# Forgetting attention with a bilinear FFN on one core: one cumulative-sum chain for the forget gates, four heads per score group in the first batch, the second batch's decay on TensorE, idle matmul steps spread through the order, weights loaded later

## The chip, the core and the metric

The kernel runs on one core of a Trainium2 chip. The metric is device time in microseconds (us) of one execution. Times of the kernel before: 422.95, 422.79 and 419.99 us, median 422.79. The engines are called by the profile's names: PE is TensorE (PEld its weight loads), DVE is VectorE, ACT is ScalarE, POOL is GpSimd, SP is SyncE, which issues most of the DMAs.

## What is computed

Eight batches (B) of eight heads (H) with 576 positions (S) of 64 values (D) go through attention with a forget gate, and the result through a bilinear FFN with 4608 tokens, width 512 and inner width 1536.

```python
scores = scale * np.matmul(q, k.transpose(0, 1, 3, 2))
log_f = np.log(np.clip(f, 0.0001, 1.0))
cum = np.cumsum(log_f, axis=-1)
decay = cum[:, :, :, None] - cum[:, :, None, :]
scores = np.where(causal, -1000000000.0, scores + decay)
scores = scores - np.max(scores, axis=-1, keepdims=True)
attn = np.exp(scores)
attn = attn / (np.sum(attn, axis=-1, keepdims=True) + 1e-09)
attn_out = np.matmul(attn, v)
x = attn_out.transpose(0, 2, 1, 3).reshape(B * S, H * D)
a = x @ w_a
b = x @ w_b
out = a * b @ w_out
```

Within a row of the softmax the term cum of the query's own position is a constant, so the kernel only subtracts cum of the key's position.

## The kernel before

**Tiles.** A pair of heads is a tile t; a batch has four, so t runs from 0 to 31, and batch b holds t = 4b to 4b + 3. Two tiles are a unit u (half a batch, four heads). The 576 query rows of a head are cut into five blocks i = 0 to 4 of 128, 128, 128, 128 and 64 rows; block i needs keys 0 to 128(i + 1). Score groups g hold blocks (1, 0), (2), (3), (4) (`groups`, L371). The inner dimension of the scores is split in two halves of 32 (dh), so that a head uses 32 rows of TensorE and four heads can lie in its four row groups at once (`RG`, L67).

**An order written by hand.** The program first builds a list of steps (`op`, L123), each with the engines that it may run on, its function, and what it depends on. `ORDER` (L961) is the order in which all steps are issued, and `CHOICE` (L1068) gives one letter for each step that has a choice of engine. An engine works its own steps in this order; semaphores hold a step until its inputs are there and its buffer is free. So a step that waits holds everything that stands behind it on its engine, the issue of DMAs on SP and POOL included.

**Start.** `constants` makes an identity on POOL. `warming` (L171) has TensorE multiply it 60 times with itself into a bank that nobody reads. `f_load` (L193) loads f twice: once as 16 rows per head group repeated over 128 partitions (the form that TensorE needs: 16 (batch, head) rows in each of eight 16-partition groups, the first two batches), once as 64 rows (all heads and batches). Each copy has its own chain: `clip` on DVE, `log` on ACT, `scan` on DVE (the cumulative sum). The first copy goes on through `high_part` and `rows_part` (L218, L221) into `crow`, fp16 rows with a high and a low part; the second is stored to DRAM by `cum_store` (L225) and read back, spread over 128 partitions, for batches 2 to 7 (`load_spread`, L450).

**Batch 0 (`DIRECT`, L69).** `first_attention` (L766) works a tile at a time. `qk_group` (L382) computes the scores of two heads with q and k, adds -cum of the key by a matmul of `pick` with `crow` (L400, L421), and the causal mask by matmuls of `low` with `neg` (L403, L427). So decay and mask are in the score bank (PSUM) when it is read: `do_max` (L478, DVE) takes the maximum of each row there, `do_exp` (L528, ACT) the exponential with the row sum, both out of the bank. There are two score tiles of two banks each (tag `sc`) and four other banks (tag `ff`) for everything else: transposes, value products, FFN.

**Batch 1.** It has the mask by matmul, too, but the decay comes from VectorE. `spread_mm` (L436) multiplies `crow` over 128 rows, `spread_ev` (L444) evicts that to SBUF (eight evictions on ACT or DVE), `spread_tail` (L447) clears its tail on POOL. `do_decay` (L483, the profile's L504) adds the spread row to the scores on DVE, takes the maximum in the same instruction and writes the sum to an SBUF tile `S`, from which `do_exp` reads. A score bank is free when the additions of its tile are done.

**Batches 2 to 7.** As batch 1, but the spread row comes by DMA and carries the mask (`mask_copy`, `mask_tail`, `mask_last` on POOL).

**After the softmax.** `do_norm` (L549, the profile's L555) scales by the reciprocal of the row sum on POOL. The probabilities are transposed, in batch 0 by TensorE (`pe_tr`, L573, evicted by `pe_tr_evict`), later by DMA; `do_pv` and `do_pv4` (L586, L616) multiply with v, `do_ev` (L627) puts the result into `xT`.

**FFN.** `ffn` (L904) takes blocks of 256 to 512 tokens. For each of 12 slices of the inner width it makes `psa` and `psb` (four matmuls each, `ff_mm` L863), copies `psa` to fp16 (`ff_copy`), multiplies (`ff_mul`, L875, DVE), and then `pso` (L881) multiplies with w_out. The FFN steps of finished batches fill TensorE between the score groups of later ones.

**Weights.** `weights` (L353) issues seven loads on POOL, which convert to fp16: columns 0 to 512 and 512 to 1536 of w_a and w_b, and three parts of w_out. Before, the first three (w_a 0, w_b 0, w_a 512) are issued within the first 5 us; the first psa runs at 52.1 us.

Of the kernel before, what the change touches and what calls it, by code (L numbers as in the profile page):

```python
# [37 lines left out]
def kernel(  # L38
# [30 lines left out]
    DIRECT = 1  # L69
    EARLY = 2  # L70
    PSPREAD = range(NP, 2 * NP)
# [99 lines left out]
    def warming(_):  # L171
        p = ps.tile([128, 512], FP32, tag="ff", bufs=RING["ff"], name="idle")
        for n in range(60):
            nc.tensor.matmul(out=p[:, 0:128], lhsT=ident, rhs=ident, start=True, stop=True)
# [3 lines left out]
    if 60:  # L178
        take(op("E", "warm", warming, [o_id], 60), "ff")
# [4 lines left out]
    NR = [128, B * H]  # L184

    def f_tiles():
        x = [s_pool.tile([128, 1024], FP32, tag="S", name=n) for n in ("cum_f", "cum_l")]
        y = spread[RING["bc"] - 1].rearrange("p h x -> p (h x)")
        cw["f"] = x[0][:, 0:S], y[0:NR[1], 0:S]
        cw["l"] = x[1][:, 0:S], y[0:NR[1], S:2 * S]  # L190
        cw["1"] = x[0][:, S:].bitcast(FP16)[:, 0:S]

    def f_load(e, m):  # L193
        rows = f.rearrange("b h s -> (b h) s")
        if m == 0:
            rows = bass.AP(rows.tensor, 0, [[0, 8], [S, 16], [1, S]])
        ENG[e].dma_start(out=cw["f"][m], in_=rows)
# [8 lines left out]
    def clip(m, lo, hi):  # L206
        x = cw["f"][m][:, lo:hi]
        nc.vector.tensor_scalar(out=x, in0=x, scalar1=1e-4, scalar2=1.0, op0=MAX, op1=MIN)

    def log(m, lo, hi):  # L210
        nc.scalar.activation(out=cw["l"][m][:, lo:hi], in_=cw["f"][m][:, lo:hi], func=LN)

    def scan(m, lo, hi):
        x = cw["f"][m]
        nc.vector.tensor_tensor_scan(out=x[:, lo:hi], data0=cw["1"][0:NR[m], lo:hi], data1=cw["l"][m][:, lo:hi],
                                     initial=x[:, lo - 1:lo] if lo else 0.0, op0=MUL, op1=SUB)

    def high_part(lo, hi):  # L218
        nc.vector.tensor_copy(out=chigh[:, lo:hi], in_=cw["f"][0][:, lo:hi])

    def rows_part(lo, hi):  # L221
        nc.vector.scalar_tensor_tensor(out=crow[:, lo:hi], in0=chigh[:, lo:hi], scalar=lsel,
                                       in1=cw["f"][0][:, lo:hi], op0=MUL, op1=ADD)

    def cum_store(_):  # L225
        nc.sync.dma_start(out=cum_d, in_=cw["f"][1])
# [4 lines left out]
    f_users = take(o_f[1], f"bc{RING['bc'] - 1}")  # L231
    o0 = op("D", "ones", f_ones)
    o_w = op("A", "table", warm_table(LN), [o0])
    crow_ops, lns = [], []
    for m, parts in ((0, ((0, 256), (256, S))), (1, ((0, S),))):
        o3 = None
        for lo, hi in parts:
            a = (m, lo, hi)
            o1 = op("D", "fclip", lambda _, a=a: clip(*a), [o_f[m]], hi - lo)
            o2 = op("A", "fln", lambda _, a=a: log(*a), [o1, o_w], hi - lo)  # L240
            o3 = op("D", "fscan", lambda _, a=a: scan(*a), [o2, o0] + ([o3] if lo else []), hi - lo)
            lns.append(o2)
            mine = [o1, o2, o3]
            if m == 0:
                o4 = op("D", "fhi", lambda _, lo=lo, hi=hi: high_part(lo, hi), [o3], hi - lo)
                o5 = op("D", "frow", lambda _, lo=lo, hi=hi: rows_part(lo, hi), [o4, o_pick], hi - lo)
                crow_ops.append(o5)
                mine += [o4, o5]
            for u in s_users:
                u.extend(mine)  # L250
            if m:
                f_users.extend(mine)
    o6 = op("S", "stc", cum_store, [o3])
    f_users.append(o6)
    o_e = op("A", "table", warm_table(EXP), lns)
    o_low = op("D", "low", lows, [o0, o_pick])
# [860 lines left out]
```

## Time and profile before

| | |
|---|---|
| median of three runs | 422.79 us |
| the profiled execution's own time | 424.4 us |
| its span, first to last instruction | 422.6 us |
| mean granted clock of TensorE | 0.947 |
| matmuls | 3712 |
| HBM read, written | 52.35 MB, 9.58 MB |

The span is what the views of the trace divide up; 1.8 us of the execution lie around it. Lines of a timeline give the start and length in us, the engine, the line of the kernel, the operation, output <- input, shapes, the count, and in brackets how long the engine stood idle before and what ended it. Rows of windows give a stretch, its length, each engine's busy time and number of instructions, the clock that TensorE was granted as a share of full speed, the share of time that the 16 DMA engines were busy, and GB/s. Rows of lines give, behind the shapes and the count, the busy time in us, the mean ns of one instruction, and the idle time before. Rows of DMAs give the size and the median us from issue to landing. Ends of matmuls are modelled, so neighbouring matmuls overlap in the rows; the distance of starts is the better measure of their cost.

### The profile page before, as it was taken

To read this page: it belongs to the slowest core of one execution; us is meant where nothing else is said; L and a number is where in the kernel's file an instruction comes from. 1 tells how busy PE (TensorE), PEld (TensorE's weight loads), DVE (VectorE), ACT (ScalarE), POOL (GpSimd) and SP (SyncE) were. 2 spreads that over 40 slices of the span, in tenths; PEclk is the share of its full clock that TensorE was granted. 3 is DMA by queue.
4 is the path that set the end of the run, shared out by engine and by line. 5 is a ranking of instruction groups with operands and counts; after the bars stand their busy time and mean duration, and the time that the engine had idled before them with its cause. 6 is when DMAs were issued, how large, how long until landed. Compare 5 with 4: busy or idle time off the path is not lost. (4 is left out here: it accounts for less than half of the span.)

```text
span 422.6 us, 10576 instructions
## 1 busy us (share of the span) xinstructions
PE 393.6 (93%) x3712; PEld 210.9 (50%) x3712; DVE 323.4 (77%) x1020; ACT 255.5 (60%) x760; POOL 257.1 (61%) x436
## 2 busy tenths in 40 slices
PE   5379999988999998999999999999899999999996
PEld 5245677565664553545445444444344444444552
DVE  3977699989899998996887799786968985452450
ACT  2867689887676856675856576387556764111121
POOL 4479688978788668876793948496775745000000
PEclk9555599999999999999999999999999999999999
DMA  8999969999999999979979897979897907300201
GB/s 239 287 201 236 185 152 279 172 293 191 211 270 200 274 208 298 251 233 180 311 158 280 188 243 233 208 194 208 253 159 237 154 31 148 109 0 2 100 2 74
DMA packets 149390, 80.85 MB, mean 191 GB/s; under 512 B 130648, under 2 KB 133208, under 8 KB 149336
## 3 DMA queue, kind: packets, MB, share of 16 engines
q1 hardware_dynamic: 145424, 75.01, 74.0%
q0 software_dynamic: 3696, 4.72, 6.8%
q8 instruction: 29, 0.48, 0.5%
q10 hardware_dynamic: 216, 0.44, 0.4%
q14 instruction: 25, 0.20, 0.1%
HBM read 52.35 MB, written 9.58 MB: 147 GB/s over the span
## 5 line engine op out<-in xcount | busy, mean ns | idle before, releaser
L504 DVE CUSTOM_DVE_ANT_0 S<-sc,spread 128x384 f32<-128x384 f32 (+4 forms) x232 | 124.0, 562 | 15.5 <-PE sc L624 5.6
L866 PE MATMUL psa<-xT,wa 128*128 128x512 f16 (+2 forms) x528 | 115.7, 342 | 1.4 <-ACT a L137 1.2
L866 PE MATMUL psb<-xT,wb 128*128 128x512 f16 (+2 forms) x528 | 115.3, 341 | 1.4 <-DVE ht L877 1.0
L555 POOL TENSOR_SCALAR PA<-PA,st 128x128 f16<-128x128 f16 (+2 forms) x180 | 83.4, 478 | 40.5 <-DVE st L547 26.6
L537 ACT ACTIVATE PA<-S,st 128x256 f16<-128x256 f32 (+2 forms) x168 | 83.9, 501 | 27.3 <-DVE st L504 26.0
L886 PE MATMUL pso<-wout,ht 128*128 128x512 f16 x432 | 98.0, 380 | 0.1
L877 DVE TENSOR_TENSOR ht<-psb,a 128x512 f16<-128x512 f32 (+2 forms) x132 | 76.2, 587 | 22.1 <-PE psb L866 17.4
L137 ACT CAST a<-psa 128x512 f16<-128x512 f32 (+2 forms) x92 | 45.4, 498 | 50.9 <-PE psa L866 46.9
L389 PE MATMUL sc<-kT,qT 32*128 32x128 f16 (+5 forms) x960 | 55.4, 284 | 20.5 <-DVE qT L300 8.0
L866 PEld LDWEIGHTS <-wb 128*128 128x128 f16 x528 | 49.8, 98 | 45.6 <-issue 6.1
L866 PEld LDWEIGHTS <-wa 128*128 128x128 f16 x528 | 49.8, 98 | 45.0 <-issue 4.9
L555 POOL TENSOR_SCALAR PB<-PB,st 128x512 f16<-128x512 f16 (+1 forms) x90 | 62.7, 710 | 15.2 <-DVE st L547 9.6
L886 PEld LDWEIGHTS <-ht 128*128 128x128 f16 x432 | 40.8, 98 | 48.9 <-DVE ht L877 1.4
L537 ACT ACTIVATE PB<-S,st 128x512 f16<-128x512 f32 x56 | 40.1, 716 | 13.0 <-DVE st L504 10.9
L389 PEld LDWEIGHTS <-qT 32*128 32x128 f16 (+1 forms) x960 | 23.5, 99 | 48.2 <-issue 24.8
L537 ACT ACTIVATION_READ_ACCUMULATOR PA<-S,st 128x1 f32 x168 | 31.7, 189 | 0.0
L457 POOL TENSOR_SCALAR_AFFINE_SELECT spread<-spread 128x768 f32<-128x768 f32 x24 | 20.7, 866 | 15.3 <-DMA spread<-cum_d 15.3
L137 ACT COPY osb<-pso 128x512 f32<-128x512 f32 x20 | 11.6, 578 | 27.2 <-PE pso L886 26.3
L533 ACT ACTIVATE PB<-S,st 128x576 f16<-128x576 f32 x28 | 21.7, 774 | 9.2 <-DVE st L504 4.4
L141 DVE CAST a<-psa 128x512 f16<-128x512 f32 (+2 forms) x40 | 23.6, 592 | 3.5 <-PE psa L866 3.1
L547 DVE RECIPROCAL st<-st 128x2 f32<-128x2 f32 x128 | 18.8, 156 | 7.7 <-ACT PB L537 4.2
L504 DVE DVE_READ_ACCUMULATOR2_ANT st<- 128x1 f32 (+1 forms) x280 | 22.9, 82 | 0.0
(98 smaller groups left out, 432.7 us busy)
## 6 DMA issues: line engine op xcount, KB each, us to landing
spread<-cum_d SPq DMA_DIRECT2D x24, 576.0 KB, 6.3
out_dram<-osb SPq DMA_DIRECT2D x36, 256.0 KB, 3.0
k<-in_k_dram SPq DMA_DIRECT2D x15, 576.0 KB, 7.3
q<-in_q_dram SPq DMA_DIRECT2D x15, 576.0 KB, 7.0
v<-in_v_dram SPq DMA_DIRECT2D x32, 256.0 KB, 7.1
wout<-in_moe_w_out_dram POOLq DMA_DIRECT2D x3, 512.0 KB, 7.6
wa<-in_moe_w_a_dram POOLq DMA_DIRECT2D x1, 1024.0 KB, 22.8
v<-in_v_dram SPq DMA_DIRECT2D x8, 128.0 KB, 4.8
```

The lines of the kernel that those rows point to most:

```text
L137: nc.scalar.copy(out=out_, in_=in_)
L141: ENG[e].tensor_copy(out=out_, in_=in_)
L389: nc.tensor.matmul(out=dst, lhsT=lhsT, rhs=rhs, start=start, stop=stop, skip_group_check=True)
L457: nc.gpsimd.affine_select(out=c[:, :, 0:SM].rearrange("p h (j k) -> p h j k", k=128), in_=c[:, :, SM:2 * SM].rearrange("p h (j k) -> p h j ...
L504: nc.vector.tensor_tensor_reduce(out=o, in0=x, in1=y, scale=-1.0, scalar=3e38, op0=ADD, op1=MIN, accum_out=m)
L533: nc.scalar.activation(out=p_blocks(t, 4), in_=T[("s" if direct else "z", t, 4)], func=EXP, bias=st[:, 8:9], scale=sign, accum_out=st[:, 1 ...
L537: nc.scalar.activation(out=p_blocks(t, i)[:, :, h, :], in_=(T[("s", t, i)][:, h, :] if direct else T[("z", t, i)][:, h * n:h * n + n]).rea ...
L547: nc.vector.reciprocal(out=st[:, 20 + 2 * i:22 + 2 * i], in_=st[:, 10 + 2 * i:12 + 2 * i])
L555: ENG[e].tensor_scalar(out=p, in0=p, scalar1=st[:, c:c + 1], scalar2=1.0, op0=MUL, op1=MUL)
L866: nc.tensor.matmul(out=p[:, 0:n], lhsT=w16[:, db, 128 * fb:128 * fb + 128], rhs=xTflat[db][:, t0:t0 + n], start=(db == 0), stop=(db == 3))
L877: nc.vector.tensor_tensor(out=ht[:, 0:n], in0=T.pop(("psb", t0, fb))[:, 0:n], in1=T.pop(("a16", t0, fb))[:, 0:n], op=MUL)
L886: nc.tensor.matmul(out=o, lhsT=T[("ht", t0, fb)][:, 128 * tb:128 * tb + 128], rhs=wout16[:, fb, :], start=(fb == 0), stop=(fb == 11))
```

## The change

1. **One chain for f.** f is loaded into one tile: 64 partitions hold the first two batches repeated, as TensorE needs them, 64 partitions all heads and batches. The first load is issued by ACT, the second by SP, behind the first k load. One chain of clip, logarithm and scan, in two column parts, serves both halves. `rows_again` copies the 64 partitions of `crow` to the other 64 (first part on POOL, second on DVE).
2. **Batch 0 by units.** `qk_group` always takes four heads. The second unit's groups 0 to 2 go to four single `ff` banks instead of the two score tiles (`single`).
3. **Batch 1 direct.** `DIRECT = 2`: its decay comes by matmul with `pick` and `crow`, its maximum by `do_max`, and its exponential reads the score bank. Spread matmuls, their evictions, the tails and the additions of batch 1 are gone.
4. **Idle steps.** `warming` is replaced by 40 steps of `filler` with four 128-column matmuls each. In the new order 18 stand before the first score group, 13 between it and the second unit's first group, and 9 singly later, the last in the FFN's second token block.
5. **A new order and choice of engines** for the whole program. The steps that the text speaks of: on POOL, the casts of the first q and `rows_again` stand ahead of the weights, which come as w_a 0, w_b 512, w_b 0, later w_a 512, and w_out; the first psa stands ahead of the first unit's group 3. On SP the v loads of batch 0 follow directly behind its q and k. The paddings go to DVE. At the first score group of batch 2 the FFN's second token block has nine slices behind it, before three (of psb two).

```diff
-    DIRECT = 1
+    DIRECT = 2
     EARLY = 2
-    PSPREAD = range(NP, 2 * NP)
+    PSPREAD = range(DIRECT * NP, EARLY * NP)
...
-    def warming(_):
+    def filler(_):
         p = ps.tile([128, 512], FP32, tag="ff", bufs=RING["ff"], name="idle")
-        for n in range(60):
-            nc.tensor.matmul(out=p[:, 0:128], lhsT=ident, rhs=ident, start=True, stop=True)
+        for n in range(4):
+            nc.tensor.matmul(out=p[:, 128 * n:128 * n + 128], lhsT=ident, rhs=ident, start=True, stop=True)
...
-    if 60:
-        take(op("E", "warm", warming, [o_id], 60), "ff")
+    for _ in range(40):
+        take(op("E", "fill", filler, [o_id]), "ff")
...
         x = [s_pool.tile([128, 1024], FP32, tag="S", name=n) for n in ("cum_f", "cum_l")]
-        y = spread[RING["bc"] - 1].rearrange("p h x -> p (h x)")
-        cw["f"] = x[0][:, 0:S], y[0:NR[1], 0:S]
-        cw["l"] = x[1][:, 0:S], y[0:NR[1], S:2 * S]
+        cw["f"], cw["l"] = x[0][:, 0:S], x[1][:, 0:S]
...
         if m == 0:
-            rows = bass.AP(rows.tensor, 0, [[0, 8], [S, 16], [1, S]])
-        ENG[e].dma_start(out=cw["f"][m], in_=rows)
+            rows = bass.AP(rows.tensor, 0, [[0, 4], [S, 16], [1, S]])
+        ENG[e].dma_start(out=cw["f"][HP[m]], in_=rows)
...
+    def rows_again(e, lo, hi):
+        ENG[e].tensor_copy(out=crow[HP[1], lo:hi], in_=crow[HP[0], lo:hi])
...
-    o_f = [op("A", "ldf", lambda e, m=m: f_load(e, m), size=m) for m in range(2)]
+    o_f = [op("AS", "ldf", lambda e, m=m: f_load(e, m), size=m) for m in range(2)]
...
+    for lo, hi in ((0, 256), (256, S)):
+        a = (lo, hi)
+        o1 = op("D", "fclip", lambda _, a=a: clip(*a), o_f, hi - lo)
+        o2 = op("A", "fln", lambda _, a=a: log(*a), [o1, o_w], hi - lo)
+        o3 = op("D", "fscan", lambda _, a=a: scan(*a), [o2, o0] + ([o3] if lo else []), hi - lo)
+        lns.append(o2)
+        o4 = op("D", "fhi", lambda _, a=a: high_part(*a), [o3], hi - lo)
+        o5 = op("D", "frow", lambda _, a=a: rows_part(*a), [o4, o_pick], hi - lo)
+        crow_ops.append(op("DP", "frow2", lambda e, a=a: rows_again(e, *a), [o5], hi - lo))
...
+    def single(u, g):
+        return u == 1 and g < 3
+
-    def qk_group(u, g, ws=(0, 1)):
+    def qk_group(u, g):
...
-        c = {w: ps.tile([128, 2, 512], FP32, tag="sc", bufs=2, name=f"sc{g}") for w in ws}
+        if single(u, g):
+            c = [[ps.tile([128, 512], FP32, tag="ff", bufs=RING["ff"], name=f"sc{g}") for _ in range(2)] for _ in range(2)]
+        else:
+            c = [ps.tile([128, 2, 512], FP32, tag="sc", bufs=2, name=f"sc{g}") for _ in range(2)]
...
-            for t in range(NP):
-                u, w = divmod(t, 2)
+            for u in range(2):
...
-                qk = op("E", f"qk{g}d", lambda _, g=g, u=u, w=w: qk_group(u, g, (w,)), deps)
-                qk_ops.setdefault((u, g), []).append(qk)
-                sc = take(qk, "sc")
+                qk = op("E", f"qk{g}d", lambda _, g=g, u=u: qk_group(u, g), deps)
+                qk_ops[(u, g)] = [qk]
...
+                if single(u, g):
+                    sc = [[take(qk, "ff") for _ in range(2)] for _ in range(2)]
+                else:
+                    sc = [[x, x] for x in (take(qk, "sc"), take(qk, "sc"))]
+                for w in range(2):
+                    softmax(2 * u + w, g, qk, sc[w], None, st_users, pu, norms)
...
-        if b < DIRECT:
+        if b == 0:
             first_attention()
```

`do_max` takes a list of two banks for the single ones, with one instruction per head there. `ORDER` and `CHOICE` are written anew.

More of the change, by code (lines that the diff above doesn't have):

```diff
@@ L232 @@
-    o0 = op("D", "ones", f_ones)
+    o_f[1].after.append(o_f[0])
+    o0 = op("D", "ones", f_ones, [])
+    o0.after.append(o_f[0])
     o_w = op("A", "table", warm_table(LN), [o0])
[L234 to L252, printed above, removed]
+    crow_ops, lns, mine = [], [], [o_f[1], o0]
@@ L425, in qk_group @@
                     for y, h, r, _ in heads:
-                        x = y[:, h, col - 128 * m:col].rearrange("p (m k) -> p m k", k=128)[:, :, 32 * a:32 * a + 32]
+                        x = y[h][:, col - 128 * m:col].rearrange("p (m k) -> p m k", k=128)[:, :, 32 * a:32 * a + 32]
                         mm(x, low[r, a, :], neg[r, :].unsqueeze(1).to_broadcast([32, m, 32]), stop=True)
-            for w in ws:
-                T[("s", t0 + w, i)] = c[w][:, :, base:col]
-        if g == 0:
-            for w in ws:
+            for w in range(2):
+                T[("s", t0 + w, i)] = [x[:, base:col] for x in c[w]] if single(u, g) else c[w][:, :, base:col]
+        if g == 0 and not single(u, g):
+            for w in range(2):
                 T[("spare", t0 + w)] = c[w][:, 0, 448:512]
@@ L480, in do_max @@
         m = st[:, 8:9] if i == 4 else st[:, 2 * i:2 * i + 2]
-        nc.vector.tensor_reduce(out=m, in_=T[("s", t, i)], axis=AXX, op=MAX, negate=True)
+        x = T[("s", t, i)]
+        for h, y in enumerate(x) if isinstance(x, list) else [(slice(0, 2), x)]:
+            nc.vector.tensor_reduce(out=m if i == 4 else st[:, 2 * i:2 * i + 2][:, h:h + 1] if isinstance(x, list) else m,
+                                    in_=y, axis=AXX, op=MAX, negate=True)
     def do_decay(t, g, i, h):
@@ L676, in softmax @@
                 if direct:
[L677 removed]
+                    mx = op("D", f"max{i}" + ("s" if sc[0] is not sc[1] else ""), lambda _, i=i: do_max(t, i), [qk])
                 else:
@@ L694, in softmax @@
                         su.append(mx)
-                sc.append(mx)
+                for x in sc if direct else sc[h:h + 1]:
+                    x.append(mx)
                 mxs.append(mx)
```

95 lines of the change are left out of this document (60 added, 35 removed), and 174 rows, old and new, of the table ORDER.

## Prediction

> **What bounds the kernel now.** I read the page first, then the engines' busy time by stretches, then the timeline of the first 90 us. The page says that TensorE is busy nearly throughout, and that for four slices of 10.6 us its granted clock is half.
>
> ```profile
> PE 393.6 (93%) x3712; PEld 210.9 (50%) x3712; DVE 323.4 (77%) x1020; ACT 255.5 (60%) x760; POOL 257.1 (61%) x436
> PEclk9555599999999999999999999999999999999999
> ```
>
> The next view gives five stretches: until the first clip of f, until the first score group of batch 1 (54.0), until the first score group of batch 2 (85.58), until a score group of batch 5 (240.74), until TensorE's end (418.7).
>
> ```profile
> 0.00:9.07 9.07, 5.64 (x60) 5.47 (x60) 2.57 (x12) 1.49 (x2) 4.48 (x15) 1.00 0.82 226
> 9.07:54.00 44.93, 32.94 (x365) 21.16 (x365) 35.10 (x67) 32.11 (x92) 28.71 (x45) 0.51 1.05 233
> 54.00:85.58 31.58, 30.84 (x477) 21.32 (x475) 30.29 (x119) 28.87 (x92) 27.52 (x45) 1.00 0.98 193
> 85.58:240.74 155.16, 149.48 (x1498) 80.41 (x1498) 134.80 (x467) 106.62 (x330) 118.29 (x199) 1.00 0.99 236
> 240.74:418.70 177.96, 174.74 (x1317) 82.53 (x1316) 120.59 (x357) 85.87 (x246) 78.11 (x134) 1.00 0.60 142
> ```
>
> Columns: stretch, length, busy time and count of PE, PEld, DVE, ACT, POOL, granted clock, DMA share, GB/s. From 85.58 on TensorE is the bound: 324.2 of 333.1 us busy. From 54 to 85.58 VectorE is (30.29 of 31.58). Before that nothing is full except, at half clock, TensorE itself: 365 matmuls in 44.93 us, against 477 in the next 31.58. That first stretch is where the change works. A closer look at it:
>
> ```profile
> 5.00:10.00 5.00, 2.01 (x28) 1.83 (x26) 0.68 (x3) 0.60 (x2) 0.29 (x1) 0.93 1.05 281
> 10.00:15.00 5.00, 0.01 (x2) 0.01 (x2) 4.93 (x9) 4.11 (x7) 0.73 (x2) 0.50 1.11 315
> ...
> 35.00:40.00 5.00, 5.00 (x47) 3.05 (x48) 3.39 (x6) 3.74 (x10) 5.00 (x10) 0.50 1.16 233
> 45.00:50.00 5.00, 5.00 (x52) 2.72 (x50) 3.36 (x11) 3.05 (x6) 4.21 (x7) 0.50 1.18 222
> 50.00:55.00 5.00, 5.00 (x93) 4.22 (x91) 4.03 (x9) 3.17 (x7) 2.84 (x4) 0.64 0.48 139
> ```
>
> The clock is granted, falls when TensorE goes idle behind its 60 warming matmuls, and comes back only between 50 and 55, though TensorE reads busy in all rows from 35 on. What differs there is the work: 128-row transposes and the first FFN matmuls instead of 32-row scores.
>
> ```profile
> 1.36 5.64 PE L174 MATMUL idle<-ident 128*128 128x128 f16 x60 [1.36 <-POOL ident masks.py:199]
> 14.99 0.60 PE L389 MATMUL sc<-kT,qT 32*128 32x256 f16 x4 [7.98 <-DVE qT L300]
> ...
> 51.30 1.03 PE L579 MATMUL psP<-ident,PB 128*128 128x128 f16 x8
> 52.13 1.06 PE L866 MATMUL psa<-xT,wa 128*128 128x256 f16 x4
> ...
> 58.55 0.89 PE L579 MATMUL psP<-ident,spread 128*128 128x128 f16 x13
> 59.38 0.62 PE L389 MATMUL sc<-kT,qT 32*128 32x384 f16 x8
> ```
>
> **The change, part by part.** I follow it to one point, the first score group of batch 2 (85.58 now), because from there both kernels do the same work in nearly the same way.
>
> *One chain for f.* It loads 64 rows twice instead of 128 and 64, and works on both at once.
>
> ```profile
> 9.07 0.53 DVE L208 TENSOR_SCALAR cum_f<-cum_f 128x256 f32<-128x256 f32 x2 [5.46 <-DMA cum_f<-in_f_dram]
> ...
> 13.38 0.43 DVE L208 TENSOR_SCALAR spread<-spread 64x576 f32<-64x576 f32 x1
> ...
> 14.78 1.29 DVE L215 TENSOR_TENSOR_SCAN spread<-cum_f,spread 64x576 f32<-64x576 f16 x1
> ```
>
> VectorE loses 0.43 + 1.29 = 1.7 us, and gains one 256-to-320-wide copy (0.25). The first clip waits for f alone (5.46 us). Half of f now goes by SP's queue directly behind k, and the weights leave the queue for the time being.
>
> ```profile
> k<-in_k_dram SPq DMA_DIRECT2D x1, 576.0 KB, 4.0
> wa<-in_moe_w_a_dram POOLq DMA_DIRECT2D x1, 1024.0 KB, 22.8
> wb<-in_moe_w_b_dram POOLq DMA_DIRECT2D x1, 512.0 KB, 19.4
> ```
>
> k lands about 4.0 us after the first issue, at 4.8; so the clip starts between 5 and 9; I take 6.2 (a quarter of k's size behind k). The first score group then needs k's and q's casts and transposes; q's go from ACT to POOL, which holds the copy of the row tables behind them, and behind that copy three weight issues:
>
> ```profile
> 4.55 0.74 POOL L363 DMA_DIRECT2D wa<-in_moe_w_a_dram  x1
> ```
>
> 2.2 us that the first v cast and the first normalizations stand behind; these need exponentials near 15, so they are covered (uncovered: up to 2.2 later value products, off the score chain). Bounds for the first score group 11 (nothing waits) and 15 (as now); I take 12.5. The three q and k loads behind the f load on SP go out one issue later, which lies in this estimate; the store of the sums moves behind a batch 1 load, and nothing reads it before batch 2. The paddings move from POOL to VectorE, into its 5.46 us of waiting: nothing.
>
> *Idle steps.* 60 warming matmuls become 40 steps of 4: 18 steps before the first score group, 13 between it and the second, 9 later. The 60 took 5.64 us, 94 ns each; one 128-column matmul costs 64 ns at full clock (13 from 58.55 to 59.38) and 104 at half (8 from 51.30 to 52.13). The first 18 end near 8, and TensorE is idle until 12.5, so the clock falls as it does now. The 13 steps are 52 matmuls, 3.3 to 5.4 us, and hold the second score group until 17 to 19.5; its k needs a landing, cast and transpose until about 16, so they cost it 1 to 3 us. In exchange they are dense 128-row work of a length that in the row of 52.13 was enough to bring the clock. I take full clock from 18 on, where it now comes at 53.
>
> The Trainium skill, "TensorE: Matmul & The Clock Gate", Part 1 (the HAM clock gate), says that about 3.4 us of sustained activity bring the full clock and one idle window of that length takes it away. The rows of 35 to 50 disagree if "activity" means a busy TensorE. By the page alone the clock would have been full from about 40 in the kernel before, and the change would be worth about 6 us less; by the rows it is worth what I count.
>
> *Four heads per score group in batch 0.* Eight groups replace sixteen. Two tiles at a time go through maxima and exponentials. With the clock up, groups 1, 2 and 3 of the first pair come at about 21, 26 and 33 (the score matmuls' 0.7 us, then the chain priced below; the last waits for the first half of w_b, third in POOL's queue, issued near 13.5 and at 19.4 us to landing). Batch 1's first group, now at 54.0, then comes at about 41, behind two more groups of 4 us each. Bounds: 37, if VectorE's work alone counts (the 35.10 of its first stretch, less 1.7 and what the list puts later, about 31, from 6.2), and 50, if only the f chain's gain reaches it.
>
> *Batch 1's decay on TensorE.* Removed: 40 decay additions, 8 evictions of spread rows (2 on VectorE), 4 small POOL fills. Added: 20 maxima and 40 short 32-row matmuls, which on TensorE stand against the 8 wide ones that made the spread rows: nothing.
>
> ```profile
> 54.00:87.00 33.00, 20.09 (x80) 1.00 0.99 194
> 9.00:52.00 43.00, 15.79 (x20) 0.50 1.07 231
> ```
>
> ```profile
> 50.21 0.68 DVE L141 COPY spread<-scd 128x512 f32<-128x512 f32 x1
> ...
> 52.98 1.20 DVE L300 STREAM_TRANSPOSE qT<-q 128x576 f32<-128x576 f32 x1
> ...
> 54.06 0.41 DVE L141 CAST a<-psa 128x256 f16<-128x256 f32 x1
> ```
>
> The first row of the upper fence is VectorE's decay line in batch 1, the second its maxima for batch 0, the same four tiles: 20.1 - 15.8 = 4.3 us saved, and 1.4 for the evictions. But the exponentials now read the score banks, and the next group waits for them. The widest group's chain:
>
> ```profile
> 62.51 0.61 PE L389 MATMUL sc<-kT,qT 32*128 32x512 f16 x8
> ```
>
> ```profile
> L481 DVE TENSOR_REDUCE st<-sc 128x2 f32<-128x1024 f32 x4 | 4.9, 1225 | 0.9 <-PE sc L389 0.8
> L537 ACT ACTIVATE PB<-sc,st 128x512 f16<-128x512 f32 x4 | 2.7, 684 | 1.1 <-DVE st L481 1.1
> ```
>
> 0.7 + 1.2 + 4 x 0.68 + 0.5 for hand-offs = 5.1 us; the narrowest, 576 columns over 64 rows, about 3.5; mean 4.6. Eight groups: 37 us where 31.6 go by now. So the point falls at 41 + 37.5 = 78.5.
>
> *Check by VectorE.* Until the point it now works 35.10 + 30.29 = 65.4 us from 9.07, and idles 11.1. The change takes 4.3 + 1.7 + 1.4 and adds 0.25, and the new list puts 7 more products, 7 more copies, a transpose and an output copy ahead of the point (14 x 0.34, the 0.41 above less an overlap of 0.07, + 1.1 + 0.7 = 6.6): 64.9. From 6.2 the point at 78.5 leaves 7.4 of idle. Less than now is plausible, because over half of it is waiting for scores at half clock:
>
> ```profile
> DVE st L481 <- PE sc L389: 5.8, 9, 1.5
> ```
>
> *FFN work pulled ahead.* At the point the new list has 18 groups of the second token block behind it, the old 5.
>
> ```profile
> 83.00 0.60 PE L866 MATMUL psa<-xT,wa 128*128 128x256 f16 x4
> 83.44 0.60 PE L866 MATMUL psb<-xT,wb 128*128 128x256 f16 x4
> 83.88 0.60 PE L866 MATMUL psa<-xT,wa 128*128 128x256 f16 x4
> 85.58 0.23 PE L389 MATMUL sc<-kT,qT 32*128 32x128 f16 x2
> 87.03 0.35 PE L624 MATMUL pv<-PTB,nv 128*64 128x64 f16 x10
> 88.42 0.39 PE L866 MATMUL psb<-xT,wb 128*128 128x256 f16 x2
> ```
>
> 13 groups at 0.44 us are 5.7; the value products of batch 1, now 87.03 to 88.42, are nearly all ahead too: 1.4. Together 7.1 us less for TensorE behind the point.
>
> *The rest.* From 85.58 to 240.74 TensorE's gaps are 5.7 us beside slightly hidden ones; VectorE has some 6 us less to do there by the entries of the list. Bounds: 4 less to 4 more stall from a new order; I take 1 less.
>
> **Sum.** 85.58 - 78.5 = 7.1, plus 7.1, plus 1: 15.2 us. The profiled execution's span is 422.6, so 407.4. That execution took 424.4, 1.8 more; the median shown is 422.79 (419.99 to 422.95). Against the median: 407.6; rounded, 408. A change under 1% (4.2 us) cannot be told from none here.
>
> **The rivals.**
> 1. *The clock falls back.* For: between 5 and 10 it fell with 2.01 of 5 us busy, and between 18 and 41 the new kernel has only about 14 us of TensorE work at full clock in 23 (half of the 32.94, less the first two groups, what the list puts later, plus the steps). Against: 9 idle steps lie in there. Price: 14 us become up to 28, 5 more than the 23; with recovery by the FFN matmuls near 38: 413.
> 2. *The chain through the score banks decides; slower.* Place: batch 1, whose groups share two score buffers that are freed only by exponentials. For: ACT and VectorE work in written order, so a maximum or exponential can stand behind a transpose (1.2), an eviction (0.7) and a product (0.4); 5.1 + 2.3 = 7.4 us a group, 59 in all, point at 100: 422.6 + 14.4 - 7.1 = 430. It decides from 6.5 us a group on. Against: VectorE's idle would have to reach 29 us. The Trainium skill, "TensorEngine Tiling (Array Packing)", PSUM Bottleneck, warns of this: packing speeds TensorE up, not the emptying of its banks.
> 3. *The weights come late.* All engines' transfers are full (DMA share 1.16), and w_b's first half now is the last of three pieces, as the piece with 22.8 us to landing is now: landing at 36.5 to 37 instead of 33, a stall of the whole order: 412.
> 4. *VectorE's lighter load counts in full*: point at 75, 3 us less stall later: 401.
> 5. *The start does not speed up*: batch 1 from 50, then 41 us of it: point at 91.5, less 7.1: 421.
>
> **How the numbers follow.** Forecast 0.50; rivals 0.17, 0.07, 0.10, 0.09, 0.07. Faster by over 1%: the forecast and rivals 1, 3, 4, 0.86; same 0.07, slower 0.07. The range reaches from rival 4 to beyond rival 1: the sum's own bounds are 3 us either way for the point, 4 for later stalls; 400 to 418 leaves out rivals 2 and 5 and little else.
>
> **What would show it.** Right: clip near 6; first score group near 12.5; granted clock 1.00 for most of 18 to 54; batch 1's first group near 41, batch 2's near 78.5; no decay or spread eviction before it; 333.1 - 7.1 us, about 326, from there to TensorE's end. Wrong: 0.50 in the rows of 25 to 40 (rival 1), ACT waiting for maxima and TensorE for exponentials of batch 1 in gaps over 2 us (rival 2), TensorE waiting for w_b (rival 3).

## The result and the profile after

The changed kernel takes 403.1 us (402.7 to 404.4) where the kernel before takes 422.9 (420.0 to 423.8): ratio 0.955, 95% interval 0.949 to 0.961. The forecast was 408. One execution of the changed kernel ran at a granted clock of 0.655, took 549.6 us and is left out; the profile read here is of another, whose own time is 404.3 us and whose span is 402.5, against 422.6 before. From the page:

```profile
PE 380.2 (94%) x3844; PEld 207.3 (52%) x3844; DVE 313.9 (78%) x959; ACT 256.6 (64%) x764; POOL 257.2 (64%) x428
PEclk9889998999999999999999999999999999999999
```

The timeline of the start, first VectorE's clip of f, then TensorE's score groups and the first psa:

```profile
7.50 0.53 DVE L205 TENSOR_SCALAR cum_f<-cum_f 128x256 f32<-128x256 f32 x2 [3.44 <-DMA cum_f<-in_f_dram]
...
12.34 0.61 PE L390 MATMUL sc<-kT,qT 32*128 32x256 f16 x8 [4.96 <-DVE qT L294]
17.50 0.50 PE L390 MATMUL sc<-kT,qT 32*128 32x256 f16 x8
21.97 0.57 PE L390 MATMUL sc<-kT,qT 32*128 32x384 f16 x8
26.50 0.39 PE L390 MATMUL sc<-kT,qT 32*128 32x512 f16 x2
31.86 0.60 PE L877 MATMUL psa<-xT,wa 128*128 128x256 f16 x4 [0.24 <-DVE xT L141]
32.83 0.86 PE L390 MATMUL sc<-kT,qT 32*64 32x512 f16 x12
39.99 0.28 PE L390 MATMUL sc<-kT,qT 32*128 32x256 f16 x2 [0.47 <-ACT spread L537]
85.28 0.53 PE L390 MATMUL sc<-kT,qT 32*128 32x128 f16 x23
```

The last two are the first score groups of batch 1 (before 54.0) and of batch 2 (85.58 before); the latter is called the point in what follows. The same five stretches as before, in the columns of the prediction's windows:

```profile
0.00:7.41 7.41, 6.01 (x72) 5.84 (x72) 2.92 (x18) 2.98 (x4) 0.70 (x6) 1.00 0.72 199
7.41:39.99 32.58, 22.73 (x447) 18.06 (x448) 30.14 (x67) 26.42 (x79) 27.00 (x41) 0.90 1.12 261
39.99:85.28 45.29, 39.97 (x623) 28.81 (x623) 37.33 (x88) 31.34 (x104) 36.01 (x58) 0.96 1.08 220
85.28:225.90 140.62, 140.01 (x1390) 73.00 (x1390) 126.63 (x441) 103.24 (x319) 112.73 (x189) 1.00 1.05 247
225.90:398.70 172.80, 171.51 (x1317) 81.61 (x1316) 116.90 (x347) 92.07 (x261) 80.75 (x137) 1.00 0.64 149
```

Here is the surprise. Batch 1 starts 14.0 us earlier, and batch 2 starts no earlier at all: the third stretch is 45.29 us long, before 31.58. Nearly all of the 20 us between the two profiles are won behind the point. From there to TensorE's end it is 333.1 us before and 313.4 now. The last stretch holds the same 1317 matmuls in both kernels and is 5.2 us shorter; the one ahead of it is 14.5 us shorter with 108 matmuls fewer, which the prediction priced at 7.1. So 7.4 + 5.2 = 12.6 us have gone from the steady state, where the prediction allowed 1. In the first of the two stretches TensorE stands idle for 0.6 us; before it was 5.7.

Where batch 1 loses its lead is seen in part in TensorE's timeline:

```profile
60.98 1.03 PE L897 MATMUL pso<-wout,ht 128*128 128x512 f16 x4
61.94 0.51 PE L390 MATMUL sc<-kT,qT 32*128 32x256 f16 x8
...
65.87 6.16 PE L897 MATMUL pso<-wout,ht 128*128 128x512 f16 x20 [3.02 <-DMA wout<-in_moe_w_out_dram]
71.97 0.50 PE L390 MATMUL sc<-kT,qT 32*128 32x384 f16 x8
```

and in the windows:

```profile
60.00:65.00 5.00, 2.84 (x55) 2.02 (x53) 4.36 (x11) 2.58 (x8) 4.82 (x7) 1.00 1.30 193
65.00:70.00 5.00, 4.13 (x12) 1.60 (x12) 2.73 (x8) 2.89 (x13) 3.04 (x6) 0.67 1.22 205
```

The output product at 65.87 waits 3.0 us for w_out, the clock falls for 3.4 us behind the wait, so that 20 wide matmuls take 6.16 us, and the next score group stands behind them: 10 us from group 0 of the second unit (61.94) to its group 1 (71.97). The larger part is work: TensorE is busy for 39.97 us of this stretch, with 623 matmuls where there were 477 (30.84 us busy). Most of what the new list pulls ahead of the point is worked here.

### The profile page after: what moved, and what is told of

The parts are those of the page before. It is cut to its first block, busy times and chain, and to the rows that moved or that the text cites. A ratio compares the mean times of both kernels' runs of the same rounds, so it can differ in the third digit from the quotient of the medians.

```text
span 547.8 us, 10783 instructions
## 1 busy us (share of the span) xinstructions
PE 534.7 (98%) x3844; PEld 248.1 (45%) x3844; DVE 320.1 (58%) x959; ACT 260.5 (48%) x764; POOL 258.7 (47%) x428
## 4 chain that ended last, share of the span: by engine, by line
PE 95%; DVE 2%; DMA 1%; ACT 1%; POOL 0%; issue 0%; SPq 0%; DVEq 0%
PE psa L877 26%; PE psb L877 26%; PE pso L897 26%; PE sc L390 9%; PE pv L604 2%; PE pv L606 1%; PE psP L584 1%; PE idle L174 1%; PE pv L616 1%; DMA cum_f<-in_f_dram 1%; PE sc L629 1%; DVE st L484 1%; PE pv L629 0%; POOL PA L560 0%; ACT spread L537 0%; ACT PA L543 0%
## 5 line engine op out<-in xcount | busy, mean ns | idle before, releaser
L877 PE MATMUL psa<-xT,wa 128*128 128x512 f16 (+2 forms) x528 | 164.3, 451 | 0.0
L877 PE MATMUL psb<-xT,wb 128*128 128x512 f16 (+2 forms) x528 | 163.9, 449 | 0.0
L897 PE MATMUL pso<-wout,ht 128*128 128x512 f16 x432 | 144.8, 511 | 0.0
L560 POOL TENSOR_SCALAR PA<-PA,st 128x256 f16<-128x256 f16 (+2 forms) x180 | 84.9, 483 | 109.5 <-DVE st L552 82.1
L508 DVE CUSTOM_DVE_ANT_0 S<-sc,spread 128x128 f32<-128x128 f32 (+3 forms) x192 | 104.1, 568 | 44.8 <-PE sc L390 38.9
L877 PEld LDWEIGHTS <-wa 128*128 128x128 f16 x528 | 61.4, 119 | 74.4 <-issue 57.5
L543 ACT ACTIVATE PA<-S,st 128x256 f16<-128x256 f32 (+2 forms) x144 | 72.1, 502 | 34.0 <-DVE st L508 33.5
L484 DVE TENSOR_REDUCE st<-sc 128x1 f32<-128x576 f32 (+8 forms) x48 | 31.4, 695 | 10.7 <-PE sc L390 9.7
L508 DVE CUSTOM_DVE_ANT_1 S<-sc,spread 128x256 f32<-128x256 f32 x48 | 19.3, 419 | 17.9 <-PE sc L390 17.8
L137 ACT CAST xT<-pv 128x512 f16<-128x512 f32 (+2 forms) x36 | 15.3, 439 | 25.4 <-PE pv L606 16.4
```

Source lines behind the costliest of these rows:

```text
L137: nc.scalar.copy(out=out_, in_=in_)
L484: nc.vector.tensor_reduce(out=m if i == 4 else st[:, 2 * i:2 * i + 2][:, h:h + 1] if isinstance(x, list) else m, in_=y, axis=AXX, op=MAX, ...
L508: nc.vector.tensor_tensor_reduce(out=o, in0=x, in1=y, scale=-1.0, scalar=3e38, op0=ADD, op1=MIN, accum_out=m)
L543: nc.scalar.activation(out=p_blocks(t, i)[:, :, h, :], in_=x.rearrange("p (j k) -> p j k", k=128), func=EXP, scale=sign, bias=st[:, c:c + ...
L560: ENG[e].tensor_scalar(out=p, in0=p, scalar1=st[:, c:c + 1], scalar2=1.0, op0=MUL, op1=MUL)
L877: nc.tensor.matmul(out=p[:, 0:n], lhsT=w16[:, db, 128 * fb:128 * fb + 128], rhs=xTflat[db][:, t0:t0 + n], start=(db == 0), stop=(db == 3))
```

## The experiments

The theory after the result was the prediction's: the early clock and the direct batch 1 bring the time, if also by other sums. The rival: neither does; the new order of the steady state does, with its choice of engines. Each was timed beside runs of the kernel before on the same chip, and each ratio is to those.

**The two kernels' own differences: clock and batch 1.**

*Repeat of the change*, unchanged.

> The changed kernel as it is, for an undisturbed profile: about 404 us. By the prediction's steps: first clip of f near 6 us, first score group near 12.5, granted clock 1.00 from about 18 on, first score group of batch 1 near 41 and of batch 2 near 78.5, some 326 us from there to TensorE's end. By rival 4: first score group of batch 2 near 75 and less stall behind it.

403.8 us (402.1 to 406.9), ratio 0.959 [0.953, 0.966]; its profile is the one above.

*Without the 13 idle steps between the first two score groups:*

```diff
-    for _ in range(40):
-        take(op("E", "fill", filler, [o_id]), "ff")
+    for n in range(40):
+        if n in mid:
+            op("E", "fill", lambda _: None, [o_id])
+        else:
+            take(op("E", "fill", filler, [o_id]), "ff")
```

> The 13 idle steps between the first two score groups issue nothing. My theory (they bring the clock early): the clock stays at half until the FFN matmuls near 35 to 40, first score group of batch 2 some 5 us later, 409 us. Rival (they only hold the second score group up, the clock is worth nothing there because VectorE sets the pace): 402 us.

404.7 us, ratio 0.960 [0.954, 0.966]: no difference that the timing shows, though the clock is half from 12.7 to 26.4 us. It was to be 409 by the prediction's reasons.

*Only the 18 idle steps at the start* (`mid` is then all the other 22):

> The changed kernel without its 13 idle steps between the first two score groups and without the 9 single ones behind them (88 matmuls in all); the 18 at the start stay. Theory A (the clock comes with the kernel's own full-height matmuls; the idle steps only shift it, and batch 0 and 1 are not bound by TensorE): 403 to 405. Rival B (the 9 steps hold the clock up while the scores alternate with waits): the clock at half for most of 25 to 54, 408 to 412.

404.3 us, ratio 0.958 [0.951, 0.964]: no difference again. Its windows, from within its first score group to batch 2's:

```profile
12.30:25.66 13.36, 7.24 (x145) 5.33 (x141) 11.22 (x30) 9.96 (x39) 10.58 (x19) 0.50 1.15 257
25.66:39.74 14.08, 11.01 (x231) 8.22 (x226) 13.77 (x31) 12.29 (x35) 13.33 (x19) 1.00 1.13 246
39.74:81.90 42.16, 37.82 (x610) 27.65 (x610) 37.35 (x88) 31.34 (x104) 36.01 (x58) 1.00 1.11 235
```

The clock is half for the first 13 us, and batch 1 starts at 39.74 all the same, where the changed kernel has 39.99. At half clock TensorE is busy for 7.24 of 13.36 us: it has room, and what goes slower holds nothing up. The clock comes back without idle steps.

*The kernel before, with 52 idle matmuls behind its second score group:*

```diff
         for o in order:
             o.fn(o.eng)
+            if o.kind == "qk0d":
+                groups_seen += 1
+                if groups_seen == 2:
+                    for _ in range(13):
+                        filler(None)
```

> The kernel before with the same 52 idle matmuls behind its second score group, nothing else changed. My theory: full clock from about 24 instead of 53, first score group of batch 1 near 46 instead of 54, 414 us. Rival (VectorE and the weights set the pace, the clock does not): the 52 matmuls hold the third score group by 3 us, 423 to 426 us.

427.0 us, ratio 1.012 [1.005, 1.020]: slower, not 7 us faster. Its windows up to the first score group of batch 2:

```profile
20.96:48.66 27.70, 22.85 (x346) 15.73 (x345) 22.68 (x49) 21.46 (x65) 22.88 (x39) 0.82 1.04 206
48.66:86.33 37.67, 31.40 (x477) 21.24 (x477) 31.56 (x122) 29.84 (x96) 30.43 (x48) 0.99 1.07 206
```

The clock is full from 21.0 to 27.8, half again until 38.0, and full from there. Against the profile of before, batch 1 starts at 48.66 in place of 54.0, and then takes 37.67 us in place of 31.58. The largest waits of TensorE, ACT and POOL in that second stretch:

```profile
PE psb L871 <- ACT osb L137: 3.7, 1, 3.7
...
ACT PB L542 <- DMA PTB<-PB: 4.8, 2, 4.3
...
POOL nv L141 <- DMA v<-in_v_dram: 5.1, 2, 2.9
```

ACT waits 4.8 us for transfers (1.2 in the same stretch of the kernel before), POOL 5.1 (0.8). But a batch 1 that starts earlier need not wait for them. In *Old up to there, new behind it* (below), whose steps are the old ones until batch 5, the clock came at 37.9 without any added matmul: batch 1 starts at 47.98 and takes 32.79 us, these two waits are 1.2 and 0.5 us, and batch 2 starts at 80.77. So the loss goes with the 52 matmuls and not with the earlier clock; by which path they cause it is not shown. The times say the same: at a mean clock of 0.968 this kernel takes 423.4 to 428.5 us, the kernel before beside it takes 418.9 to 421.8 in its five executions at 0.966 and 0.967.

*The kernel before, with batch 1 direct and nothing else* (the steps that are gone leave the order, and the exponentials of a group stand ahead of the next group, since they free the banks):

```diff
-    DIRECT = 1
+    DIRECT = 2
...
-        if b < DIRECT:
+        if b == 0:
             first_attention()
```

> The kernel before with batch 1's decay on TensorE alone (additions become maxima in the same places, spread matmuls, evictions and tails gone, exponentials of a group ahead of the next group). My theory: VectorE's 5.7 us are given back by the chain through the score banks, which takes 37 instead of 31.6 us: 420 to 425 us. Rival (VectorE's load counts): 5 to 6 us less, 417 us. Rival 2 of the prediction (chain of 7 us a group): over 440 us.

429.8 us, ratio 1.019 [1.013, 1.026]: 9 us slower by the medians, 6.3 us by the spans of the two profiles, whose clocks are alike (428.9 and 422.6 us, 0.948 and 0.947). It is more than the theory's 425 and less than rival 2's 440. Batch 1 in its windows, and TensorE's waits there:

```profile
53.30:94.79 41.49, 32.59 (x512) 23.06 (x512) 27.08 (x61) 27.63 (x91) 27.66 (x43) 1.00 0.85 181
```

```profile
PE sc L389 <- ACT PA L537: 5.8, 6, 2.3
PE sc L389 <- ACT PB L537: 2.8, 4, 1.3
```

VectorE is relieved (27.08 us, 30.29 before) and the stretch is 10 us longer, because score groups and parts of groups wait ten times, 8.6 us in all, for the exponentials that free their banks. That is the chain through the score banks: 41.49 / 8 = 5.2 us a group, where the forecast had 4.6 and rival 2 had 7.4.

**The steady state.** Both kernels have the same TensorE work left at the first score group of batch 5 (1317 matmuls), so there the two orders can be cut and joined.

*Old up to there, new behind it* (step numbers of the old kernel, where the orders part; the letters of `CHOICE` for the moved part go along):

```diff
-        ... 2005 1101 1137 1149 2001 2008 1132 1997 1129 1096 ...
+        ... 2005 1101 1137 1050 1129 1997 1096 1139 1149 1194 ...
```

> The kernel before up to the first score group of batch 5 (240.74 us there), from there on the steps in the changed kernel's order and with its choice of engines. TensorE has the same work left at that group in both kernels; it then took 178.0 us before and 172.8 us after the change. Theory A (the new steady-state order and engines themselves hold TensorE less, wherever one comes from): 5 us less, about 415.5, with some 173 us from that group to TensorE's end. Rival B (the changed kernel is faster behind the first two batches because of the state in which these leave it: FFN slices, normalizations and loads further ahead): no change, about 420.5 and 178 us.

*New up to there, old behind it:*

```diff
-        ... 1095 1136 1133 1143 1188 1189 2000 1097 1096 1126 ...
+        ... 1095 1136 1133 1042 1226 1143 1995 2002 1126 1128 ...
```

> The changed kernel up to the first score group of batch 5 (225.90 us there), from there on the order and the choice of engines of the kernel before. Theory A (the new order and engines themselves hold TensorE less): 5 us are lost, about 409, with 178 us from that group to TensorE's end. Rival B (the state in which the first batches leave the kernel): no change, about 404 and 173 us.

The first takes 414.0 us, ratio 0.984 [0.978, 0.989], the second 412.5, ratio 0.977 [0.968, 0.986]; the kernel before beside them 420.0. Their last stretch, first the old start with the new end, then the reverse:

```profile
236.63:408.02 171.39, 171.17 (x1317) 81.55 (x1316) 116.87 (x347) 91.58 (x258) 78.06 (x134) 1.00 0.62 148
```

```profile
225.21:407.21 182.00, 176.32 (x1317) 83.31 (x1316) 120.86 (x358) 87.62 (x249) 80.73 (x137) 0.99 0.59 142
```

171.4 and 182.0 us, where the unmixed kernels have 172.8 (new) and 178.0 (old). The stalls go with the order and the engines of that stretch, wherever the kernel comes from: theory A holds in the main. The 182.0 us are 4.0 more than the old kernel needs there, so the joint costs something too: TensorE waits 2.2 us for DMAs that transpose probabilities, which it does not in the old kernel, and the clock falls once (0.99).

**Order or engines?** *The changed kernel with the old engine for all 89 steps behind the point whose letter differs* and *the kernel before with the new ones (94)*, the orders left as they are (the end of `CHOICE` of each):

```diff
-        ...DAAAAAAADAAAAAAAADAAADAAADDAAADAAAAADADADAAADAAADDADAAADADAA
+        ...AAAAAAADADADDAAAAADDAADAAADDAADDADDDAAAADAADAADDAADAAADAAADA
```

```diff
-        ...AAAAAAADADADDAAAAADDAADAAADDAADDADDDAAAADAADAADDAADAAADAAADA
+        ...DAAAAAAADAAAAAAAADAAADAAADDAAADAAAAADADADAAADAAADDADAAADADAA
```

> The changed kernel with the old choice of engine for all steps behind the first score group of batch 2; its order stays. 9 output copies and 9 small transposed copies go back from ACT to VectorE, about 8 us of work by the rows of both traces. Theory A1 (within the new order it is the choice of engines, VectorE relieved of evictions, that takes the stalls away): most of 12 us come back, about 412 to 416. Theory A2 (it is the order): about 404, at most 406.

> The kernel before with the new choice of engine for all steps behind the first score group of batch 2; its order stays. Theory A1 (the choice of engines takes the stalls away): 409 to 413. Theory A2 (the order does): about 420, since the choice was made for another order perhaps more.

417.4 us, ratio 0.989 [0.981, 0.998], and 428.0, ratio 1.012 [1.002, 1.022]. From the point to TensorE's end the traces give:

| us from the first score group of batch 2 | old engines | new engines |
|---|---|---|
| old order | 333.1 | 336.8 |
| new order (7.1 us less to do there, by the prediction's count) | 326.5 | 313.4 |

The windows of the two mixed kernels, first the new order with the old engines, then the reverse:

```profile
82.99:230.68 147.69, 142.65 (x1389) 74.03 (x1389) 129.18 (x447) 101.41 (x313) 112.86 (x189) 1.00 1.02 235
230.68:409.48 178.80, 174.52 (x1317) 81.89 (x1316) 121.60 (x358) 87.97 (x249) 80.77 (x137) 1.00 0.62 144
```

```profile
86.27:244.18 157.91, 151.14 (x1498) 80.44 (x1498) 132.97 (x461) 108.10 (x335) 118.03 (x198) 1.00 0.99 231
244.18:423.11 178.93, 174.92 (x1317) 82.92 (x1316) 115.51 (x347) 90.44 (x257) 78.15 (x134) 1.00 0.59 141
```

The new order alone wins its 7.1 us and nothing more (333.1 - 326.5 = 6.6), the new engines alone lose 3.7, and together they take away 12.6 beside the 7.1. Neither has that gain; the fit of the two has.

**Which engine choices?** *The old choice for the output copies alone* (21 letters of `CHOICE`, 9 more copies on VectorE) and *the old choice for all the others* (68 letters):

```diff
-        ...DAAAAAAADAAAAAAAADAAADAAADDAAADAAAAADADADAAADAAADDADAAADADAA
+        ...DAAAAAAADDADDAAAADAAADAAAADDAADAAAAADADADAADAAAADDADAAADAADA
```

```diff
-        ...DAAAAAAADAAAAAAAADAAADAAADDAAADAAAAADADADAAADAAADDADAAADADAA
+        ...AAAAAAADAAAAAAAAAADDAADAADDAAADDADDDAAAADAAADADDAADAAADAADAA
```

> The changed kernel with the old choice of engine for the output copies alone, behind the first score group of batch 2: 15 go from ACT to VectorE, 6 the other way, so VectorE gets 9 more, 9 x 0.69 = 6.2 us. Theory A1 (VectorE's load as such sets the stalls): about two thirds of the 13 us that the whole old choice cost, 412 to 413. Theory A3 (order and choice fit together step by step; each step that goes to the engine that is busy at that place costs, whichever kind it is): about half, 409 to 411, and the other half of the choice costs as much.

> The changed kernel with the old choice for everything behind the first score group of batch 2 but the output copies: 24 copies of psa go from VectorE to ACT and 24 the other way, the small copies net 8 to VectorE (some 2 us). Theory A1 (VectorE's load as such): 2 us of 8 come back to it, so 406 to 408. Theory A3 (order and choice fit together step by step): 409 to 413, though VectorE's load hardly changes.

405.0 us, ratio 0.960 [0.951, 0.968], and 415.0, ratio 0.983 [0.976, 0.990]. Neither theory had this: the output copies cost nothing, the rest nearly all. The windows behind the point, first of the output copies' kernel, then of the other:

```profile
83.92:226.05 142.13, 140.96 (x1389) 73.33 (x1389) 129.35 (x446) 100.91 (x314) 112.46 (x189) 1.00 1.04 245
226.05:398.81 172.76, 171.90 (x1317) 81.56 (x1316) 119.23 (x351) 90.26 (x256) 80.76 (x137) 1.00 0.64 149
```

```profile
84.94:231.55 146.61, 142.25 (x1390) 73.73 (x1390) 126.32 (x442) 103.67 (x318) 112.72 (x189) 1.00 1.02 237
231.55:408.68 177.13, 173.65 (x1317) 81.86 (x1316) 119.35 (x354) 89.79 (x253) 80.93 (x137) 1.00 0.63 146
```

VectorE works 129.35 + 119.23 = 248.6 us behind the point in the first and 126.32 + 119.35 = 245.7 in the second, which takes 10 us longer. Its load is not what decides. What differs is seen in VectorE's products by lines, first in the changed kernel, then with the old choice:

```profile
L888 DVE TENSOR_TENSOR ht<-psb,a 128x512 f16<-128x512 f32 (+2 forms) x113 | 69.2, 617 | 20.2 <-PE psb L877 17.2 <-ACT a L137 0.8 <-DVE st L552 0.4
```

```profile
L888 DVE TENSOR_TENSOR ht<-psb,a 128x512 f16<-128x512 f32 (+2 forms) x113 | 69.1, 617 | 22.5 <-PE psb L877 15.0 <-ACT a L137 5.9
```

The products wait 0.8 us in all for ACT's copies of psa in the one, 5.9 in the other, and everything behind them on VectorE waits with them. There 24 copies of psa stand on ACT that the new choice puts on VectorE, and 24 the other way round: their number is the same, their places are not.

On TensorE's side the loss lies in the score matmuls, the same 768 behind the point in both kernels. Their rows, first of the kernel before, then of the changed one:

```profile
L389 PE MATMUL sc<-kT,qT 32*128 32x128 f16 (+4 forms) x768 | 33.7, 262 | 6.1 <-DVE st L504 3.4 <-DVE xT L141 1.4 <-DVE st L547 0.4
L390 PE MATMUL sc<-kT,qT 32*128 32x128 f16 (+4 forms) x768 | 28.9, 261 | 0.4 <-DVE st L508 0.4
```

Busy and idle together they fall by 10.5 us, from 39.8 to 29.3, which is of the size of the 12.6. Of the 6.1 us idle before, 3.4 are ended by VectorE's decay additions (`st`, L504), which free the score banks. The four kernels of the new order fall in line:

| us behind the point | changed | old output copies | old rest | all old engines |
|---|---|---|---|---|
| products wait for ACT's copies | 0.8 | 1.2 | 5.9 | 6.2 |
| score matmuls, busy + idle ahead of them | 28.9 + 0.4 | 30.0 + 0.7 | 32.2 + 4.3 | 33.2 + 5.4 |
| to TensorE's end | 313.4 | 314.9 | 323.7 | 326.5 |

That late copies make the additions late, and these the score groups, is read from these waits and was not tried by itself. The 20 small copies of value products (`xT`) have a part in it: of the 4.3 us idle, 1.8 wait for such a copy on VectorE, and none in the changed kernel.

**A better version?** *w_out one place earlier:*

```diff
-        ... 273 86 262 164 166 ... 222 207 208 90 82 180 281 ... 1651 298 1650 88 229 ... 1660 1663 89 306 ...
+        ... 273 86 90 262 164 166 ... 222 207 208 88 82 180 281 ... 1651 298 1650 89 229 ... 1660 1663 306 ...
```

(86 is the second half of w_a; 90, 88, 89 are the parts of w_out.)

> The changed kernel with the three loads of w_out one place earlier each on POOL's queue (the last is issued near 46 in place of 55.05). In the changed kernel the first product with w_out waits 3.0 us for them, and the clock falls for 3.4 us behind that wait. Theory A (that wait holds batch 1): the first score group of batch 2 at 81 to 82, 3 to 4 us less in all, 400 to 401. Rival B (batch 1 goes by the chain through its score banks, and the wait lies beside it): first score group of batch 2 near 85, 403 to 404.

402.4 us (400.8 to 404.3), ratio 0.953 [0.946, 0.961]; span 399.6, 2.9 less than the changed kernel's. Its windows from batch 1 to batch 5:

```profile
41.12:81.27 40.15, 38.37 (x622) 28.31 (x621) 37.44 (x88) 31.62 (x104) 35.02 (x57) 1.00 1.22 240
81.27:222.77 141.50, 140.35 (x1391) 73.23 (x1391) 126.82 (x441) 102.89 (x319) 112.86 (x189) 1.00 1.06 245
```

The wait for w_out and the half clock are gone, and batch 1 takes 40.15 us, not 45.29: the wait was on the path, and the point is where theory A had it. Against the changed kernel's own median (403.8) the gain is 1 us, not 3 to 4, and the intervals of the two overlap: the profile shows it, the timing alone does not.

What then holds batch 1 is TensorE's own work, 38.37 of 40.15 us. All its waits there:

```profile
PE sc L390 <- ACT spread L537: 0.9, 2, 0.5
PE pv L616 <- DMA xT<-PA: 0.8, 2, 0.6
PE pv L616 <- DVE a L141: 0.2, 1, 0.2
```

The chain through the score banks, which costs the old kernel 8.6 us of waiting, costs at most 0.9 here. More other work stands between the score groups now: 622 matmuls in the stretch, where the old kernel with a direct batch 1 has 512.

## Why the prediction was right, and where it was not

The time was right by two errors that cancelled: 6.8 us too much gain ahead of the point, 11.6 too little behind it. That they nearly cancel is luck.

- *f, first score group, second group*: 7.50, 12.34 and 17.50, predicted 6.2 (5 to 9), 12.5 and 17 to 19.5. Right.
- *Groups of the first pair and batch 1's start*: 21.97, 26.50, 32.83 and 39.99; predicted 21, 26, 33 and 41. Right in the times, wrong in the reason. "With the clock up" was not needed: without the 13 steps the groups ran at half clock to 25.66 and batch 1 came at 39.74. And of the 14.0 us, 6.0 lie in the execution that is compared: where the old steps had the clock from 37.9 on, batch 1 came at 47.98 and not at 54.0. The other 8.0 are left to the f chain, the four heads per group and the new order of loads; these were not tried one by one.
- *Batch 1 direct*: "Eight groups: 37 us where 31.6 go by now. So the point falls at 41 + 37.5 = 78.5." This step failed, in its mechanism and in its size; batch 1 took 45.29 us, and the point fell at 85.28. It was costed by the chain through the score banks, 4.6 us a group. In the old kernel that chain is there (5.2 us a group, and the direct batch 1 alone is a loss of 6 to 9 us), but in the changed one it hardly makes TensorE wait. TensorE's own work fills the stretch: 38.37 us busy with w_out earlier, 30.84 before. The sum took 7.1 us of FFN groups and value products off behind the point and charged them nowhere ahead of it; 9 of the 13 groups and 56 matmuls of value products more than before stand in this stretch. It also put the short `pick` matmuls at nothing, and they are 3.4 us, where the spread and `pick` matmuls were 1.5. Its check was made for VectorE alone. The rest, 45.29 - 40.15 = 5.1, is mostly the wait for w_out (3.0) and the half clock behind it (6.16 - 4.49 = 1.7). The prediction looked at the late weights in w_b (rival 3), which landed in time, and not at the transfer that came last. The Trainium skill, "TensorEngine Tiling (Array Packing)", PSUM Bottleneck, warned that the emptying of the banks does not speed up with packed matmuls. The old kernel with a direct batch 1 agrees (8.6 us of waits for ACT); the changed kernel's batch 1 was not held by it.
- *FFN pulled ahead*: 108 matmuls fewer behind the point; the new order with the old engines shows it in time, 6.6 against 7.1. What it costs ahead of the point was left out, as said.
- *The rest*: "Bounds: 4 less to 4 more stall from a new order; I take 1 less." This step failed in size: 12.6. It costed the order as a list of work per engine and looked for gaps in TensorE's row, 5.7 us; slightly hidden waits were named and not counted. By PE busy and idle, the last stretch alone went from 174.74 busy and 3.2 idle to 171.51 and 1.3 with the same matmuls: more than half of what the new order and engines saved there was inside "busy". The ends of matmuls are modelled, which may be why; that is not shown.
- *Rival 4* gave 401 us, and named "VectorE's lighter load": near in time, wrong in the cause; the kernel with 9 output copies more on VectorE is as fast.
- *Rival 1* (the clock falls back) came true in part: it fell at 22.3 for 3.4 us and again at 66.7. Its price was nil in batch 0, where TensorE has room, and 1.7 us in batch 1, behind the wait for w_out.

The Trainium skill, "TensorE: Matmul & The Clock Gate", Part 1, was weighed as worth 6 us less, with the clock of the kernel before full from about 40. The profiled execution does not agree (53.6), the other execution of its steps does (37.9), and there the point comes at 80.77 and not at 85.58. So which of the two one starts from moves the worth of the change by some 5 us. In the changed kernel it does not matter: with 13 us of half clock and with less it takes the same time (404.3 and 403.8).

## What to carry to other kernels

Cost a rewritten order at the place where it holds the bounding engine, not by the sums per engine: here the order alone and the engines alone gave nothing of the 12.6 us, and both together gave them. By the waits, what counts is which of two engines holds a copy at the moment its reader needs it. Work that is pulled ahead of a point must be charged ahead of it, on the engine that does it. A stage that starts earlier gains only if the load that lands last in it comes earlier too. And before a clock is counted as gain, see whether TensorE has room in that stretch even at half speed, and which clock the execution had that one compares with.

## What was not expected of the hardware

- The kernel before does not find its clock at the same time in each execution: in the profile of before it is half until 53.6 us, in the run with the old start and the new end, whose steps are the same up to there, until 37.9; batch 1 then starts at 47.98 in place of 54.0, and batch 2 at 80.77 in place of 85.58. It shows in the times: of the 27 executions of the kernel before beside the experiments, the 14 with a mean clock of 0.966 or 0.967 took 418.0 to 421.8 us, the 11 with 0.944 to 0.951 took 422.7 to 426.7. No run shows what decides between the two.
- A gap of 3 us in TensorE can cost a stretch of half clock, and need not. Five profiled kernels have the same steps up to batch 2. Behind waits for w_out of 2.45 us (new up to batch 5, old behind it), 2.94 (old rest of the choice) and 3.02 (changed) the clock was half for 3.4 us, and the 20 wide matmuls took 6.16 us; behind 1.88 (old output copies) and 3.20 (all old engines) it stayed, and they took 4.48. With w_out earlier the granted clock is 1.00 throughout batch 1.
- The clock record of these traces changes in multiples of 3.41 us: half for 3.41 us (changed kernel, three times), 13.65 (18 idle steps only), 27.31 (old start, new end) and 44.37 (before).
